# A decode block on one core: one load fewer for the first MLP weights, the last load of the second MLP weights cut in two

## The chip, the core and the metric

The kernel runs on one core of a Trainium2 chip. The core has a matrix engine (TensorE, PE in the rows), VectorE (DVE), ScalarE (ACT), GpSimd (POOL), a queue that issues transfers (SyncE, SP) and 16 DMA engines that move data from the chip's memory (HBM) into the on-chip buffer (SBUF). The metric is the time of one execution in device microseconds (us), as a median of several runs.

## The reference

One token for each of four sequences goes through attention over a window of the key and value cache, and then through an MLP; all data are float32.

```python
# x: (4, 1, 448); 16 query heads on 8 cached heads of width 256; the last 1024 cached positions
h  = x + attention(layernorm(x), k_cache, v_cache, wq, wo)
y  = layernorm(h)
g  = gelu(y @ w1 + b1)        # w1: (448, 1792)
h2 = h + (g @ w2 + b2)        # w2: (1792, 448)
```

## The kernel before

All caches and weights are packed by the host into a few wide arrays of 128 rows, one row for each SBUF partition, and are read once. The SP queue issues 23 loads in a fixed order (and one store at the end); the engines follow the data. Twelve wide loads, `stream0` to `stream11`, carry queries' weights, keys, values and output weights of the eight cached heads, in the order of the table `LOADS`, through a ring of three buffers. For each head the kernel projects the query, multiplies it with the keys (`scores`), takes the softmax, multiplies with the values (`values`), and adds the head's share of the output projection.

In the last pass of the loop over heads (`g == HKV - 1`) the last loads are issued: the last head's values `v7` in two parts, the output weights of the last two heads (`wo67`) and `w1` in three parts into the tile `tw`, and `w2` in four parts into the tile `tw2`. Each part has its own semaphore (DMAHW0 to DMAHW7 in turn), and an instruction that reads a part waits for that part's semaphore.

The tail of the program, after the attention, is a chain. The first layer is done in four steps `a` = 0 to 3 over 128 rows of `w1` each (the last step has 64 rows, and its weights lie side by side): `pu` collects `zT` times `w1`. `u` is then scaled, taken through the GELU on ScalarE, transposed into `put` and `gT`. The second layer runs over 14 chunks `c` of `w2`, 128 rows by 448 columns each: `py` collects `gT[:, c]` times chunk `c`. At the end `res` adds `py` and the rest, and `out` is stored.

TensorE's program order is written by hand. The weight parts before the change are: `w1` columns for `a` = 0 and 1 (1792 KB), for `a` = 2 (896 KB), for `a` = 3 (448 KB); `w2` chunks 0 to 7 (1792 KB), 8 to 10 (672 KB), 11 and 12 (448 KB), 13 (224 KB). `W1C` is `3 * F + F // 2` columns, `F` is 1792, `D` is 448, `H` is 64. Matmuls named `idle` (`keep_warm`) use constant data and only keep TensorE occupied.

Of the kernel before, what the change touches and what calls it, by code (L numbers as in the profile page):

```python
# [15 lines left out]
B, D = 4, 448  # L16
# [3 lines left out]
F = 1792  # L20
P = 128
H = P // 2
# [41 lines left out]
W1C = 3 * F + F // 2  # L64
# [1 line left out]
SCALE = DH ** -0.5  # L66

@with_exitstack
def block_kernel(ctx: ExitStack, tc, rows, first, streams, v7, wo67, w1, w2, out):
    nc = tc.nc  # L70
    const = ctx.enter_context(tc.tile_pool(name="const", bufs=1))
    ring = ctx.enter_context(tc.tile_pool(name="ring", bufs=3))
# [10 lines left out]
    def slot(name):  # L83
        return ring.tile([P, SLOT], F32, tag="t", name=name)
# [4 lines left out]
    def part(kind, g, i=0):  # L89
        while (kind, g, i) not in held:  # L90
            src = streams.pop(0)
            t = slot("stream")
            wanted = LOADS[len(LOADS) - len(streams) - 1]
            if src is streams_first:
                nc.sync.dma_start(t[:, : WC + X0], first)
            at = WC + X0 if src is streams_first else 0
            nc.sync.dma_start(t[:, at : at + src.shape[-1]], src)
            at = 0
            for one in wanted:
                held[one] = t[:, at : at + width(one)]  # L100
                at += width(one)
        return held[kind, g, i]

    def wq_parts(t):
        parts = [(a, a, slice(0, 512), t[:, a * 512 : (a + 1) * 512]) for a in range(3)]
        for i in range(2):
            parts.append((3, 3 + i, slice(i * 2 * P, (i + 1) * 2 * P), t[:, 3 * 512 : 4 * D]))
        return parts

    def wo_rows(t):  # L110
        return t.rearrange("p (j e) -> p j e", j=4)
# [11 lines left out]
    def load_v7():  # L123
        t = slot("v7")
        for a, b in ((0, V7A), (V7A, KV)):
            nc.sync.dma_start(t[:, a:b], v7[:, a:b])
        return chunk_pairs(t[:, :KV])
# [68 lines left out]
    def project_q(g, parts):  # L196
        pq = ps_m.tile([P, 512], F32, tag="m", name=f"pq{g}")
        for j, a, cols, w in parts:
            nc.tensor.matmul(pq[j * Q : (j + 1) * Q, cols], yT[:, a, :], w, start=True, stop=True)  # L199
        qs = work.tile([P, 512], F32, tag="qs", name=f"qs{g}")  # L200
        nc.scalar.copy(qs, pq)  # L201

        pt = ps_m.tile([P, 2 * REP, B], F32, tag="m", name=f"pqt{g}")
        for i in range(2 * REP):
            nc.tensor.matmul(pt[:, i, :], qs[:, i * P : (i + 1) * P], sel[:, :B], start=True, stop=True)  # L205

        src = pt.rearrange("p (r c) b -> p c b r", r=REP)
        for i in range(2):
            nc.vector.tensor_copy(qT[g % 2][:, :, :, i * REP : (i + 1) * REP], src)  # L209

    def scores(g):
        s = [ps_s.tile([P, 512], F32, tag="s", name=f"s{g}_{h}") for h in range(2)]
        if g == HKV - 1:
            keep_warm(12, s[0])
        mx = work.tile([P, 2], F32, tag="mx", name=f"mx{g}")
        for h in range(2):
            for c in range(2):
                for b in range(B):
                    nc.tensor.matmul(  # L219
                        s[h][b * Q : (b + 1) * Q, :], qT[g % 2][:, c, b, :], load_k(g, h, c)[:, b, :],  # L220
                        start=(c == 0), stop=(c == 1),
                    )
            nc.vector.reduce_max(mx[:, h : h + 1], s[h], axis=AX.X)  # L223
        nm = work.tile([P, 1], F32, tag="nm", name=f"nm{g}")
        nc.vector.tensor_max(nm, mx[:, 0:1], mx[:, 1:2])
        nc.vector.tensor_scalar_mul(nm, nm, -SCALE)  # L226
        p = work.tile([P, 2 * 512], F32, tag="p", name=f"p{g}")
        sums = work.tile([P, 2], F32, tag="sums", name=f"sums{g}")
        for h in range(2):
            nc.scalar.activation(  # L230
                p[:, h * 512 : (h + 1) * 512], s[h], AF.Exp, bias=nm, scale=SCALE,
                accum_out=sums[:, h : h + 1],
            )
        rec = work.tile([P, 1], F32, tag="rec", name=f"rec{g}")
        nc.vector.tensor_add(rec, sums[:, 0:1], sums[:, 1:2])
        nc.vector.reciprocal(rec, rec)
        return p, rec

    def transpose_p(g, p):
        pt = ps_t.tile([P, NKC, P], F32, tag="t", name=f"ppt{g}")  # L240
        if g == HKV - 1:
            keep_warm(8, pt.rearrange("p c k -> p (c k)"))
        for c in range(NKC):
            nc.tensor.transpose(pt[:, c, :], p[:, c * P : (c + 1) * P], ident)  # L244

        src = pt.rearrange("p (c i) (b q) -> p c i b q", i=2, b=B)
        for i in range(2):
            nc.vector.tensor_copy(pT[g % 2][:, :, :, i * REP : (i + 1) * REP], src[:, :, i, :, :REP])  # L248


    def values(g, v7=None):
        po = ps_o.tile([P, 2, DH], F32, tag="o", name=f"po{g}")
        for c in range(NKC // 2):
            vt = load_v(g, c) if v7 is None else v7[c]
            for b in range(B):
                nc.tensor.matmul(  # L256
                    po[b * Q : (b + 1) * Q], pT[g % 2][:, c, b, :], vt[:, :, b, :],
                    start=(c == 0), stop=(c == NKC // 2 - 1),
                )
        return po  # L260
# [5 lines left out]
    def columns(t, j):  # L266
        if j < 3:
            return t[:, j * P : (j + 1) * P].rearrange("p (i c) -> p i c", i=2)
        return t[:, None, 3 * P :].to_broadcast([t.shape[0], 2, H])
# [49 lines left out]
    def keep_warm(n, to=None):  # L319
        to = tail[0][:, 0, :] if to is None else to  # L320
        for _ in range(n):
            nc.tensor.matmul(to[:Q, :512], idle[:, :Q], idle, start=True, stop=True)  # L322
# [5 lines left out]
    for g in range(HKV):  # L328
        if g + 1 < HKV:
            p, rec_next = scores(g + 1)  # L330
            if g + 2 < HKV:
                project_q(g + 2, wq_parts(part("q", g + 2)))
            transpose_p(g + 1, p)
            if g + 1 == HKV - 2:
                keep_warm(8, ps_m.tile([P, 512], F32, tag="m", name="wait"))
            if g + 1 == HKV - 1:
                tail.append(ps_t.tile([P, 2, 512], F32, tag="t", name="tail"))
                accs = once.tile([P, D], F32, tag="u", name="accs")
                nc.scalar.copy(accs, acc)
                keep_warm(10)  # L340
                hsum = ps_s.tile([P, 512], F32, tag="s", name="hsum")[:, :P]
                ph = hsum.rearrange("p (i c) -> p i c", i=2)
                pu = ps_s.tile([P, 512], F32, tag="s", name="pu")[:, :FQ]
                for j in range(4):
                    nc.tensor.matmul(ph[j * Q : (j + 1) * Q], sel, columns(accs, j), start=True, stop=False)
        else:
            v7t = load_v7()
            tw = slot("w1")
            wo_last = [wo_rows(tw[:, i * WC : (i + 1) * WC]) for i in range(2)]
            nc.sync.dma_start(tw[:, : 2 * WC], wo67)  # L350
            tw1 = tw[:, 2 * WC : 2 * WC + W1C]
            for a, n in ((0, 2 * F), (2 * F, F), (3 * F, F // 2)):
                nc.sync.dma_start(tw1[:, a : a + n], w1[:, a : a + n])
            tw2 = slot("w2")
            for c0, n in ((0, 8), (8, 3), (11, 2), (13, 1)):
                nc.sync.dma_start(tw2[:, c0 * D : (c0 + n) * D], w2[:, c0 * D : (c0 + n) * D])
        if g == HKV - 1:
            keep_warm(4)
        po = values(g, v7t if g == HKV - 1 else None)
        heads(g, po, rec)  # L360
        if g < HKV - 2:
            project_o(g, wo_rows(part("o", g)))
        if g == HKV - 1:
            keep_warm(3)
            for i in range(2):
                project_o(HKV - 2 + i, wo_last[i])
        if g + 1 < HKV:
            rec = rec_next
# [5 lines left out]
    def w1_part(a, j):  # L374
        if a < 3:
            return slice(0, P), w1t[a][:, FQ * j : FQ * (j + 1)]
        rows = slice(H * (j // 2), H * (j // 2) + H)
        return rows, w1t[a][rows, FQ * (j % 2) : FQ * (j % 2 + 1)]
# [36 lines left out]
    for a in range(ND):  # L415
        for j in range(4):
            rows, w = w1_part(a, j)
# [27 lines left out]
    for c in range(NFC):  # L445
        for j in range(4):
            n = 2 if c == 0 or j < 3 else 1
# [79 lines left out]
```

## Time and profile before

| | before |
|---|---|
| median of 3 runs | 214.74 us (214.71 to 214.75) |
| the profiled execution's own time | 214.74 us |
| its span, first to last instruction | 212.9 us |
| PE busy | 148.6 us, 70% of the span |
| DVE, ACT, POOL busy | 33.5, 24.0, 5.6 us |
| DMA | 88.52 MB, mean 416 GB/s |
| chain that ended last | DMA 80%, PE 16%, DVE 1%, ACT 1% |

The profiled execution took as long as the median of the runs; 1.8 us of it lie outside the span. The chain that ended last is followed back from the last instruction to what each step waited for. Its line for DMA means that for 80% of the span the step that counted was a transfer on its way.

### The profile page before, as it was taken

What the parts mean: (1) busy time and instruction counts of PE and PEld (TensorE: products, weight loads), DVE (VectorE), ACT (ScalarE), POOL (GpSimd) and SP (SyncE); (2) the same over time, 40 slices, a digit from 0 to 9 for tenths busy, and PEclk for the clock granted to TensorE, in tenths of its full rate; (3) what the DMA queues carried; (4) which work ended last, traced back from release to release, by engine and by line L of the source; (5) the groups of instructions that cost most, each with busy time, mean ns of one, the idle gap of its engine ahead of it and who ended that gap; (6) DMA issues with size and microseconds to landing.
All of it is one profiled execution on the core that took longest, in us unless ns stands there. A gap on an engine that the chain in (4) does not pass through costs nothing.

```text
span 212.9 us, 2617 instructions
## 1 busy us (share of the span) xinstructions
PE 148.6 (70%) x1143; PEld 65.5 (31%) x1143; DVE 33.5 (16%) x138; ACT 24.0 (11%) x57; POOL 5.6 (3%) x17
## 2 busy tenths in 40 slices
PE   0476815842894895870798770687989898999984
PEld 0342311400421512330324130152352434426453
DVE  1410310400103100310104110031130031101220
ACT  1110300300002100210003000030030102000310
POOL 6100000000000000000000000000000000000110
PEclk9999985995559669997559996599699999999999
DMA  7999798999989999999999989999999999999991
GB/s 299 429 420 508 339 508 370 469 435 407 488 356 484 434 413 440 395 481 398 455 455 392 455 384 478 425 425 392 473 402 413 449 422 416 420 413 415 434 380 64
DMA packets 3499, 88.52 MB, mean 416 GB/s; under 512 B 400, under 2 KB 656, under 8 KB 1312
## 3 DMA queue, kind: packets, MB, share of 16 engines
q1 hardware_dynamic: 3456, 88.31, 96.9%
q8 instruction: 9, 0.15, 0.3%
q10 hardware_dynamic: 32, 0.05, 0.1%
q14 instruction: 2, 0.02, 0.0%
HBM read 88.29 MB, written 0.07 MB: 415 GB/s over the span
## 4 chain that ended last, share of the span: by engine, by line
DMA 80%; PE 16%; DVE 1%; ACT 1%; issue 1%; SPq 0%; ACTq 0%
DMA stream<-stream 60%; DMA w<-w 10%; DMA v<-v 9%; PE po L256 6%; PE s L219 4%; PE acc L293 1%; PE pot L281 1%; PE pq L199 1%; PE ppt L244 1%; DVE o L273 1%; ACT o L274 1%; PE pqt L205 1%; PE py L449 0%; ACT qs L201 0%; DVE oT L288 0%
## 5 line engine op out<-in xcount | busy, mean ns | idle before, releaser
L219 PE MATMUL s<-stream,qT 128*32 128x512 f32 x256 | 40.8, 788 | 18.6 <-DMA stream<-stream 18.6
L256 PE MATMUL po<-stream,pT 128*32 128x512 f32 x224 | 30.6, 685 | 15.6 <-DMA stream<-stream 15.4
L219 PEld LDWEIGHTS s<-stream,qT 128*32 128x32 f32 x256 | 10.5, 141 | 46.2 <-issue 33.7
L223 DVE TENSOR_REDUCE mx<-s 128x1 f32<-128x512 f32 x16 | 11.1, 692 | 63.7 <-PE s L219 63.7
L256 PEld LDWEIGHTS po<-stream,pT 128*32 128x32 f32 x224 | 7.2, 120 | 32.5 <-DMA stream<-stream 18.1
L281 PE MATMUL pot<-ident,o 128*128 128x8 f32 x64 | 11.3, 287 | 4.7 <-DVE o L273 3.7
L199 PE MATMUL pq<-stream,yT 128*32 128x512 f32 (+1 forms) x80 | 9.8, 582 | 6.0 <-DMA stream<-stream 3.1
L281 PEld LDWEIGHTS pot<-ident,o 128*128 128x128 f32 x64 | 9.9, 223 | 13.0 <-DVE o L273 11.3
L205 PE MATMUL pqt<-sel,qs 128*128 128x4 f32 x64 | 9.6, 274 | 6.0 <-ACT qs L201 6.0
L201 ACT COPY qs<-pq 128x512 f32<-128x512 f32 x8 | 4.7, 585 | 77.5 <-PE pq L199 77.5
L230 ACT ACTIVATE p<-s,nm 128x512 f32<-128x512 f32 x16 | 10.9, 688 | 17.4 <-DVE nm L226 17.4
L273 DVE TENSOR_SCALAR o<-po,rec 128x256 f32<-128x256 f32 x8 | 3.9, 484 | 53.8 <-PE po L256 53.8
L205 PEld LDWEIGHTS pqt<-sel,qs 128*128 128x128 f32 x64 | 8.9, 216 | 10.3 <-ACT qs L201 10.3
L274 ACT ACTIVATE o<-po,rec 128x256 f32<-128x256 f32 x8 | 3.8, 474 | 69.2 <-DVE o L273 69.2
L244 PE MATMUL ppt<-ident,p 128*128 128x128 f32 x64 | 9.8, 299 | 0.4 <-ACT p L230 0.4
L293 PE MATMUL acc<-stream,oT 128*32 128x448 f32 x48 | 7.6, 708 | 2.2 <-DVE oT L288 1.4
L322 PE MATMUL tail<-idle 128*32 128x512 bf16 x33 | 8.5, 381 | 0.4 <-DVE pT L248 0.4
L322 PEld LDWEIGHTS <-idle 128*32 128x32 bf16 x67 | 5.8, 96 | 9.3 <-issue 3.9
L244 PEld LDWEIGHTS ppt<-ident,p 128*128 128x128 f32 x64 | 8.1, 162 | 1.4 <-ACT p L230 1.1
L199 PEld LDWEIGHTS pq<-stream,yT 128*32 128x32 f32 x80 | 4.2, 122 | 13.6 <-issue 12.3
L193 POOL TENSOR_TENSOR r<-ve_r,mhalf 128x1 f32<-128x1 f32 x2 | 1.1, 542 | 191.8 <-DVE ve_r L192 191.8
L209 DVE COPY qT<-pqt 128x16 f32<-128x16 f32 x16 | 2.0, 170 | 17.6 <-PE pqt L205 17.6
(98 smaller groups left out, 70.0 us busy)
## 6 DMA issues: line engine op xcount, KB each, us to landing
stream<-stream SPq DMA_DIRECT2D x5, 7040.0 KB, 40.4
stream<-stream SPq DMA_DIRECT2D x2, 6912.0 KB, 39.8
stream<-stream SPq DMA_DIRECT2D x2, 4992.0 KB, 25.0
stream<-stream SPq DMA_DIRECT2D x2, 4096.0 KB, 24.1
stream<-stream SPq DMA_DIRECT2D x1, 5888.0 KB, 34.4
w<-w SPq DMA_DIRECT2D x2, 1792.0 KB, 23.1
v<-v SPq DMA_DIRECT2D x1, 3072.0 KB, 19.8
w<-wo SPq DMA_DIRECT2D x1, 1792.0 KB, 20.1
```

The costliest lines, as they stand in the source:

```text
L199: nc.tensor.matmul(pq[j * Q : (j + 1) * Q, cols], yT[:, a, :], w, start=True, stop=True)
L205: nc.tensor.matmul(pt[:, i, :], qs[:, i * P : (i + 1) * P], sel[:, :B], start=True, stop=True)
L219: nc.tensor.matmul(s[h][b * Q : (b + 1) * Q, :], qT[g % 2][:, c, b, :], load_k(g, h, c)[:, b, :], start=(c == 0), stop=(c == 1),)
L223: nc.vector.reduce_max(mx[:, h : h + 1], s[h], axis=AX.X)
L230: nc.scalar.activation(p[:, h * 512 : (h + 1) * 512], s[h], AF.Exp, bias=nm, scale=SCALE, accum_out=sums[:, h : h + 1],)
L244: nc.tensor.transpose(pt[:, c, :], p[:, c * P : (c + 1) * P], ident)
L256: nc.tensor.matmul(po[b * Q : (b + 1) * Q], pT[g % 2][:, c, b, :], vt[:, :, b, :], start=(c == 0), stop=(c == NKC // 2 - 1),)
L273: nc.vector.tensor_scalar_mul(o[:, 0], po[:, 0], rec)
L274: nc.scalar.mul(o[:, 1], po[:, 1], rec)
L281: nc.tensor.matmul(pt[:, c], o[:, i, c * P : (c + 1) * P], rows_of_pair[:, i * REP : (i + 1) * REP, :], start=(i == 0), stop=(i == 1),)
L293: nc.tensor.matmul(acc[i * Q : (i + 1) * Q, :], oT[g % 2][:, i, :], wt[:, i, :], start=(g == 0), stop=(g == HKV - 3),)
L322: nc.tensor.matmul(to[:Q, :512], idle[:, :Q], idle, start=True, stop=True)
```

## The change

The second and third part of `w1` become one load. The last part of `w2` (chunk 13) becomes two loads: its rows 0 to 63 from `w2` as before, and its rows 64 to 127 from a new array `w2e`, in which the host has laid these 64 rows as 8 blocks of 8 rows with an unused ninth row behind each block. The number of loads stays 23, and the bytes read stay the same.

```diff
-            for a, n in ((0, 2 * F), (2 * F, F), (3 * F, F // 2)):
+            for a, n in ((0, 2 * F), (2 * F, W1C - 2 * F)):
                 nc.sync.dma_start(tw1[:, a : a + n], w1[:, a : a + n])
             tw2 = slot("w2")
-            for c0, n in ((0, 8), (8, 3), (11, 2), (13, 1)):
+            for c0, n in ((0, 8), (8, 3), (11, 2)):
                 nc.sync.dma_start(tw2[:, c0 * D : (c0 + n) * D], w2[:, c0 * D : (c0 + n) * D])
+            nc.sync.dma_start(tw2[:H, 13 * D : 14 * D], w2[:H, 13 * D :])
+            nc.sync.dma_start(tw2[H:, 13 * D : 14 * D], w2e[:, :8, :])
...
+    w2e = np.concatenate([w2[H:, 13 * D :].reshape(8, 8, D), np.zeros((8, 1, D), np.float32)], axis=1)
```

On the SP queue, from the output weights to the end, the loads before were (`w_896` is the tile of `wo67` and `w1`, `w_901` that of `w2`; the shape is partitions by float32 elements, in brackets what the issue waits for):

```order
L350 DMA w_896<-wo 128x3584 [waits DMAHW4_49,PE_49]
L353 DMA w_896<-w 128x3584
L353 DMA w_896<-w 128x1792
L353 DMA w_896<-w 128x896
L356 DMA w_901<-w 128x3584 [waits DMAHW5_49,PE_49]
L356 DMA w_901<-w 128x1344
L356 DMA w_901<-w 128x896 [waits DMAHW6_49]
L356 DMA w_901<-w 128x448 [waits DMAHW7_49]
```

and with the change (`w_900` is the tile of `w2`):

```order
L350 DMA w_896<-wo 128x3584 [waits DMAHW4_49,PE_49]
L353 DMA w_896<-w 128x3584
L353 DMA w_896<-w 128x2688
L356 DMA w_900<-w 128x3584 [waits DMAHW5_49,PE_49]
L356 DMA w_900<-w 128x1344
L356 DMA w_900<-w 128x896
L357 DMA w_900<-w 64x448 [waits DMAHW6_49]
L358 DMA w_900<-w2e 64x1x448 [waits DMAHW7_49]
```

One issue is gone behind the first part of `w1`, all of `w2` moves up by one place, and two loads of 64 partitions stand at the end, with the waits that the two last loads had before.

On TensorE's queue, in the first layer, steps `a` = 2 and `a` = 3 of `pu` before, each with a wait of its own:

```order
L382 MATMUL tail<-zv,fold 128x1 [waits DVE_49,Activation_49]
L418 MATMUL pu<-w_896,zT 32x448 [waits DMAHW2_49]
L418 MATMUL pu<-w_896,zT 32x448 x3
L418 MATMUL pu<-w_896,zT 32x448 [waits DMAHW3_49]
L418 MATMUL pu<-w_896,zT 32x448 x3
```

and with the change:

```order
L384 MATMUL tail<-zv,fold 128x1 [waits DVE_49,Activation_49]
L420 MATMUL pu<-w_896,zT 32x448 [waits DMAHW2_49]
L420 MATMUL pu<-w_896,zT 32x448 x7
```

All eight matmuls now stand behind one wait, that for the joined load. Further on, the end of `py` on TensorE's queue before, from chunk 11 to the last chunk:

```order
L449 MATMUL py<-w_901,gT 32x128 [waits DMAHW6_49]
L449 MATMUL py<-w_901,gT 32x128 x2
L449 MATMUL py<-w_901,gT 32x64
L449 MATMUL py<-w_901,gT 32x128 [waits DVE_49]
L449 MATMUL py<-w_901,gT 32x128 x2
L449 MATMUL py<-w_901,gT 32x64
L449 MATMUL py<-w_901,gT 32x128 [waits DMAHW7_49]
L449 MATMUL py<-w_901,gT 32x128 x2
L449 MATMUL py<-w_901,gT 32x64
```

and with the change:

```order
L451 MATMUL py<-w_900,gT 32x128 [waits DMAHW5_49]
L451 MATMUL py<-w_900,gT 32x128 x2
L451 MATMUL py<-w_900,gT 32x64
L451 MATMUL py<-w_900,gT 32x128 [waits DVE_49]
L451 MATMUL py<-w_900,gT 32x128 x2
L451 MATMUL py<-w_900,gT 32x64
L451 MATMUL py<-w_900,gT 32x128 [waits DMAHW7_49,DMAHW6_49]
L451 MATMUL py<-w_900,gT 32x128 x2
L451 MATMUL py<-w_900,gT 32x64
```

The last chunk waits for two loads in place of one; nothing else on TensorE, VectorE, ScalarE or GpSimd changes its place.

## Rows read from the trace of the kernel before

**Rows 1.** Chain that ended last, its last pieces: start us, us, what.

```profile
187.47 21.49 DMA w<-w
208.96 0.04 issue
209.00 1.05 PE py L449 x12
210.05 0.02 issue
210.07 0.29 DVE res L453
```

**Rows 2.** Timeline of TensorE's weight loads in the second layer, 201 to 210.6 us.

```profile
206.28 2.36 PEld L449 LDWEIGHTS py<-w,gT 128*32 128x32 f32 x88 [0.76 <-issue]
209.00 0.37 PEld L449 LDWEIGHTS py<-w,gT 128*32 128x32 f32 x16 [0.35 <-DMA w<-w]
209.58 0.16 PEld L449 LDWEIGHTS py<-w,gT 128*32 128x32 f32 x8 [0.21 <-DMA w<-w]
```

**Rows 3.** Windows: per stretch PE, PEld, DVE, ACT, POOL busy, PEclk, DMA share, GB/s.

```profile
200.00:202.00 2.00, 2.00 (x20) 0.91 (x20) 0.38 (x2) 0.14 (x1) 0.54 (x1) 1.00 1.00 414
206.00:206.80 0.80, 0.49 (x22) 0.52 (x25) 0.14 (x1) 0.00 (x0) 0.00 (x0) 1.00 1.02 408
207.00:207.40 0.40, 0.40 (x24) 0.40 (x18) 0.00 (x0) 0.00 (x0) 0.00 (x0) 1.00 0.70 273
207.60:208.00 0.40, 0.40 (x25) 0.40 (x19) 0.00 (x0) 0.00 (x0) 0.00 (x0) 1.00 0.54 211
208.00:208.60 0.60, 0.60 (x30) 0.60 (x24) 0.00 (x0) 0.00 (x0) 0.00 (x0) 1.00 0.50 188
209.00:209.40 0.40, 0.40 (x16) 0.37 (x16) 0.00 (x0) 0.00 (x0) 0.00 (x0) 1.00 0.00 0
```

**Rows 4.** DMA queues: packets, MB, share of 16 engines' span.

```profile
q1 hardware_dynamic: 3456, 88.31, 96.9%
q8 instruction: 9, 0.15, 0.3%
```

**Rows 5.** Timeline of SP: start us, us, issues of the last loads, one window each.

```profile
174.53 1.38 SPq L353 DMA_DIRECT2D w<-w  x3
...
175.00 0.90 SPq L353 DMA_DIRECT2D w<-w  x2
...
183.95 0.80 SPq L356 DMA_DIRECT2D w<-w  x2
...
187.47 2.81 SPq L356 DMA_DIRECT2D w<-w  x2
...
189.95 0.33 SPq L356 DMA_DIRECT2D w<-w  x1
```

**Rows 6.** The same loads, one window each: KB, us from issue to landing.

```profile
w<-w SPq DMA_DIRECT2D x1, 1792.0 KB, 24.0
w<-w SPq DMA_DIRECT2D x1, 896.0 KB, 25.7
w<-w SPq DMA_DIRECT2D x1, 448.0 KB, 26.4
...
w<-w SPq DMA_DIRECT2D x1, 1792.0 KB, 22.2
w<-w SPq DMA_DIRECT2D x1, 672.0 KB, 23.5
...
w<-w SPq DMA_DIRECT2D x1, 448.0 KB, 21.5
w<-w SPq DMA_DIRECT2D x1, 224.0 KB, 19.6
```

**Rows 7.** Timeline, first layer's steps 2 and 3, 201.2 to 203.6 us.

```profile
201.29 0.30 PEld L382 LDWEIGHTS tail<-zv,fold 128*128 128x128 f32 x2 [0.73 <-issue]
201.60 0.16 PEld L418 LDWEIGHTS pu<-w,zT 128*32 128x32 f32 x8
202.49 0.15 PEld L418 LDWEIGHTS pu<-w,zT 64*32 64x32 f32 x8 [0.73 <-DMA w<-w]
203.51 0.48 DVE L431 SCALAR_TENSOR_TENSOR u<-pu,r,rs 128x256 f32<-128x256 f32 x1 [0.45 <-PE pu L418]
```

**Rows 8.** Timeline, VectorE's last copies before the second layer.

```profile
205.80 0.34 DVE L443 COPY gT<-put 64x8 f32<-64x8 f32 x2
```

**Rows 9.** Instructions of line 449: duration ns min/median/max, first and last start.

```profile
L449 PEldq EVENT_SEMAPHORE  x1: 51/51/51, 206.2 to 206.2; - x1
```

More of the change, by code (lines that the diff above doesn't have):

```diff
@@ L68, in block_kernel @@
 @with_exitstack
-def block_kernel(ctx: ExitStack, tc, rows, first, streams, v7, wo67, w1, w2, out):
+def block_kernel(ctx: ExitStack, tc, rows, first, streams, v7, wo67, w1, w2, w2e, out):
     nc = tc.nc
@@ L511 @@
         "rows": rows, "first": first, **streams, "v7": v[-1], "wo67": np.concatenate([wo[-2], wo[-1]], axis=1), "w1": w1, "w2": w2,
+        "w2e": w2e,
     }
```

## The prediction

> **What bounds the kernel now.** I read the chain that ended last first: its final link is a load of `w2` weights that lands at 208.96 us, then 1.05 us of TensorE in the second layer, then VectorE's `res` at 210.07 [rows 1]. So the end is set by the last weight loads, and the timeline of TensorE's weight loads shows by how much [rows 2]: 88 loads (chunks 0 to 10; 8 to a chunk) run from 206.28 without a pause that counts and end at 208.65 (209.00 less the 0.35 us that the engine then sat idle for a load); 16 (chunks 11, 12) go from 209.00 to 209.37; after 0.21 us of idleness the last 8 (chunk 13) begin at 209.58, when the last load has landed. Two waits of 0.35 and 0.21 us are all that the last loads cost TensorE. That 0.21 us, and a little of the 0.35, is what the change can win.
>
> Next I read the DMA share in narrow stretches of the tail [rows 3]. It is 1.00 and 1.02 until 206.8 us, 0.70 at 207.0 to 207.4, 0.54 at 207.6 to 208.0, 0.50 from 208.0 to 208.6, and 0.00 from 209.0. A share of 0.50 is 8 of 16 engines: half of them finish at about 207 to 208, the other half work on to about 209.0, and these alone decide when the last loads land. A reason that fits stands among the queues: besides the data there are nine packets of instructions, which took 0.3% of 16 engines' span, so 0.003 x 16 x 212.9 / 9 = 1.1 us of one engine each [rows 4]. One such packet on each of eight engines would make them late by about as much as is seen.
>
> The times of landing come from the issues and their us to landing [rows 5, 6]. `w1`: steps 0 and 1 at 174.53 + 24.0 = 198.53; step 2 at 175.00 + 25.7 = 200.70; step 3 at 175.47 (the end of the three issues, 175.91, less one issue of about 0.43) + 26.4 = 201.87. `w2`: 183.95 + 22.2 = 206.15; about 184.35 + 23.5 = 207.85; 187.47 + 21.5 = 208.97; 189.95 + 19.6 = 209.55. The last two agree with the ends of TensorE's waits.
>
> **The change, step by step.**
>
> *One load less in `w1`.* The differences of those landings price a load: 896 KB took 2.17 us, 448 KB took 1.17 and 1.12, 224 KB took 0.58. Twice 1.12 less 2.17 is 0.07 us that a load costs whatever its size; from 1.17 it would be 0.17, from 0.58 against 1.12 it is 0.04. I take 0.07 (0.04 to 0.17). The joined load lands at 201.80, and all of `w2` lands 0.07 earlier: chunks 0 to 7 at 206.08, chunks 11 and 12 at 208.90. Nothing changes for SP: the moved issues keep their waits, stand 18 us and more ahead of their landings, and the two last keep the places of the two last.
>
> *A wait for step 2.* Before, its weights landed at 200.70, ahead of TensorE, which came to them at 201.60 after the two weight loads of the `zv` mean [rows 7]. Now they land with step 3's at 201.80; 0.04 us pass from a landing to the start [rows 1], so step 2 starts at 201.84, 0.24 us late (with no saving by the joined load 0.31; never below nothing). Behind it stand step 3, whose own weights were there, and then `u`: VectorE took it up at 203.51, when `pu` was done [rows 7], so `u`, the GELU, `put` and `gT` all move by 0.24. `gT`'s last copy ended at 206.14 [rows 8], and TensorE began `py` at 206.28; that becomes 206.52, its weights being there at 206.08.
>
> *Where that goes.* The 88 loads of chunks 0 to 10 take 2.37 us, so they end at 208.89. Chunks 11 and 12 are there at 208.94 (208.90 and 0.04). The idle 0.35 us has swallowed the delay, with 0.05 to spare. Were that cover gone, each further tenth would be paid at the end. The 16 loads then end at 208.94 + 0.37 = 209.31, against 209.37 before.
>
> *The last chunk.* Its 224 KB took 0.58 us on 16 engines. Rows 0 to 63 go as half the bytes with the whole fixed cost, about (0.58 - 0.07) / 2 + 0.07 = 0.33. Rows 64 to 127, if eight engines share them, are as many rows for each of the eight as the whole load had before: 0.58 on these eight, nothing on the others. No row says which eight are late. If the late eight are the ones that get nothing of rows 64 to 127, they are done at 208.90 + 0.33 = 209.23 (before 209.55). The early eight ended their data by 208.0; less 0.07 and 0.26, plus 0.58, that is 208.25, and with the half microsecond between the end of the data at 209.0 and the landing at 209.55 they land at 208.8. So chunk 13 is there at 209.23, earlier than TensorE, which comes at 209.31. Its first matmul now waits for two loads: a semaphore wait of its own took 51 ns on this queue [rows 9], at most 0.05 more. I take 209.36 for the start, against 209.58: 0.22 us earlier. From there the 8 loads, `res`, the store and the end are as before.
>
> The sum: 214.74 - 0.22 = **214.52 us**, made against the profiled execution, whose own time equals the median of the runs.
>
> Bounds of this case: with 0.17 for the fixed cost chunks 11 and 12 start at 208.84, end at 209.21, and without the semaphore's 0.05 the gain is 0.37 (214.37). With 0.04, the step-2 delay is 0.27, `py`'s 88 loads end at 208.92, the next start at 208.97 and end at 209.34, and with the semaphore's 0.05, and as much again for anything the split costs on top, the gain is 0.14 (214.60).
>
> A rule that speaks against the second edit: the Trainium skill, "DMA: Bandwidth & Descriptors", Rules for kernel authors, advises against two transfers to disjoint partition halves, because both run over all 16 engines and so serialize; one load of 128 partitions is better. By it the last chunk would cost 0.33 twice instead of 0.58. No run here shows it. The same page (Why a DMA increments its semaphore by 16 and not by 1) lets the engines be counted by the largest number up to 16 that divides the slowest dimension on both sides, here 64 and 8, so 8, the lowest-numbered ones; no row here shows that either.
>
> **The rivals.**
>
> *The late eight, or one of them, share rows 64 to 127.* Slower. One late engine is enough, since the chunk waits for the last. They land at 208.90 + 0.33 + 0.58 = 209.81, chunk 13 starts at 209.85, 0.27 later than now (0.28 with 0.04 as the fixed cost, 0.22 with 0.17, and 0.05 more with the semaphore's wait). The time is 215.01 (214.96 to 215.07). For it: nothing in the profile names the engines. Against it: if the lateness comes from queues of their own, as the packets of instructions suggest, the late eight may well be one block, and then it is wholly the one block or the other. The point that decides: whether an engine still busy at 208.6 has rows of the second part.
>
> *The eight blocks run over all 16 engines.* The change then does not do what it says. The halves cost 0.33 each, and the chunk lands at 208.90 + 0.66 = 209.56, as before, whatever the fixed cost, since one is saved and one added: 214.75 (214.80 with the semaphore's wait). The rule on halves of the Trainium skill's page "DMA: Bandwidth & Descriptors", above, would make it this. Against it stands only that the two sides of the second load are cut differently, 64 rows on one, 8 blocks on the other.
>
> *One engine moves all 64 rows.* 0.58 us for 8 rows is about 0.07 a row, so 64 take 4.6 us. An early engine starts them by 208.0 - 0.33, ends at 212.3 and lands at about 212.8, a late one a microsecond later: 3.3 to 4.3 us on the end, 218.0 to 219.0. Nothing in the rows speaks for it; no load before had blocks on one side and rows on the other.
>
> **How the numbers follow.** Forecast (late eight relieved): 0.53; it is a judgement of the two blocks, not a reading. Late ones loaded: 0.30. All 16: 0.10. One engine: 0.04. Something the rows don't show: 0.03. The likeliest gives 214.52, with a range of its own from 214.37 to 214.60. Forecast and first rival together have no more than 0.83, so the range for 8 in 10 takes in both: 214.37 to 215.08. A measurement of this kernel can tell about 0.2% (0.43 us) from no change. Forecast, first rival and second all lie inside that; only one engine, and part of the unseen, lie outside. The unseen and a stronger gain than the bounds give faster 0.06, the single engine and a worse delay slower 0.08, and the same 0.86.
>
> **What would show it.** Right: DMA share falls from 0.5 to nothing a quarter of a microsecond earlier; TensorE's wait before the last 8 loads of `py` is under 0.06; step 2 waits for `w1` by about a quarter of a microsecond and the idleness before chunk 11 shrinks from 0.35 to about 0.05. Wrong: the last wait grows to about 0.5, with a share of 0.5 or less to past 209.2 (late ones loaded); a share of 0.06 for microseconds (one engine); no idleness before chunk 11 and a later `py` (the joined load costs more than its cover). It would also fail if a different half were late in another execution.

## The result and the profile after

The change makes the kernel slower: 215.29 us as median of 11 runs (215.21 to 215.57), against 214.75 (214.65 to 215.44) for the kernel before on the same chip; the ratio is 1.0025 [1.0017, 1.0033]. That is 0.54 us more, where I forecast 0.22 less, and outside my range (to 215.08).

The profiled execution of the changed kernel took 215.33 us. Its chain ended last in this way (start us, us, what):

```profile
207.41 3.30 PE py L451 x66
210.71 0.02 issue
210.73 0.29 DVE res L455
```

Against [rows 1], `res` comes 0.66 us later, and the load has gone from the chain: TensorE now seems to be the bound. Its timeline of weight loads says the same, against [rows 2]:

```profile
202.99 0.16 PEld L420 LDWEIGHTS pu<-w,zT 128*32 128x32 f32 x8
...
207.38 3.02 PEld L451 LDWEIGHTS py<-w,gT 128*32 128x32 f32 x112 [0.46 <-issue]
```

This is a trap. The first layer runs 1.4 us late (202.99 against 201.60 in [rows 7]), so all 112 loads of `py` find their weights there. In this execution TensorE's granted clock stood at half of its full level for some microseconds from 187.6 us on (last section). Executions of the kernel before with as low a mean clock (0.840 to 0.848, where the others have about 0.86) took 215.45 to 215.51 us (four of them), those of the change 215.33 to 215.57 (three): as far as these few tell, the two kernels don't differ with that stretch, so TensorE's rows of this trace can't show what the change did. A second profile of the same kernel, without that stretch, shows it (run `ra_change_again`; timeline of weight loads, and of `res`):

```profile
201.87 0.16 PEld L420 LDWEIGHTS pu<-w,zT 128*32 128x32 f32 x8 [0.23 <-DMA w<-w]
...
206.26 1.71 PEld L451 LDWEIGHTS py<-w,gT 128*32 128x32 f32 x64 [0.46 <-issue]
208.33 0.59 PEld L451 LDWEIGHTS py<-w,gT 128*32 128x32 f32 x24 [0.36 <-DMA w<-w]
209.61 0.62 PEld L451 LDWEIGHTS py<-w,gT 128*32 128x32 f32 x24 [0.70 <-DMA w<-w]
...
210.55 0.29 DVE L455 TENSOR_TENSOR res<-py,hb 128x128 f32<-128x128 f32 x1 [4.14 <-PE py L451]
```

Read it against [rows 2]. Chunks 8 to 10, which ran on without a wait before, now wait 0.36 us for their load. Chunks 11 and 12 start at 209.61, not 209.00. Chunk 13, the one whose load was cut, no longer waits at all: the last 24 loads go in one piece. So the time was lost on loads that the change doesn't touch, ahead of the cut one. The windows of the same profile answer to [rows 3] (columns as there):

```profile
206.00:206.80 0.80, 0.51 (x22) 0.54 (x26) 0.40 (x3) 0.00 (x0) 0.00 (x0) 1.00 1.02 408
207.00:207.40 0.40, 0.40 (x24) 0.40 (x17) 0.00 (x0) 0.00 (x0) 0.00 (x0) 1.00 0.86 211
207.60:208.00 0.40, 0.40 (x22) 0.37 (x13) 0.00 (x0) 0.00 (x0) 0.00 (x0) 1.00 0.51 148
208.00:208.60 0.60, 0.51 (x22) 0.27 (x17) 0.00 (x0) 0.00 (x0) 0.00 (x0) 1.00 0.62 224
209.00:209.40 0.40, 0.18 (x6) 0.00 (x0) 0.00 (x0) 0.00 (x0) 0.00 (x0) 1.00 0.46 135
```

At 207.0 the engines are busier than before (0.86 against 0.70) and move less (211 GB/s against 273). Busy share times 16 counts the busy engines; GB/s over that count tells at what pace each of them runs. That is 211 / (0.86 x 16) = 15.3 GB/s for each, against 273 / (0.70 x 16) = 24.4 before; at 207.6 it is 18.1 against 24.4. The engines are slower than before.

### The profile page after: what moved, and what is told of

It is laid out like the page before. It is cut to its first block, busy times and chain, and to the rows that moved or that the text cites. A ratio compares the mean times of both kernels' runs of the same rounds, so it can differ in the third digit from the quotient of the medians.

```text
span 213.5 us, 2618 instructions
## 1 busy us (share of the span) xinstructions
PE 150.6 (71%) x1143; PEld 66.2 (31%) x1143; DVE 33.5 (16%) x138; ACT 24.1 (11%) x57; POOL 5.6 (3%) x17
## 4 chain that ended last, share of the span: by engine, by line
DMA 58%; PE 34%; another core or an unknown queue 3%; DVE 1%; ACT 1%; issue 1%; SPq 0%; ACTq 0%
DMA stream<-stream 49%; PE s L219 9%; DMA v<-v 9%; PE po L256 8%; PE pot L281 3%; PE acc L293 3%; PE tail L322 2%; PE pu L420 2%; PE py L451 2%; PE pq L199 1%; PE pqt L205 1%; DVE o L273 1%; PE ppt L244 1%; PE hsum L299 1%
## 5 line engine op out<-in xcount | busy, mean ns | idle before, releaser
L219 PE MATMUL s<-stream,qT 128*32 128x512 f32 x256 | 38.5, 749 | 16.9 <-DMA stream<-stream 16.9
L256 PE MATMUL po<-stream,pT 128*32 128x512 f32 x224 | 32.3, 721 | 17.1 <-DMA stream<-stream 17.0
L219 PEld LDWEIGHTS s<-stream,qT 128*32 128x32 f32 x256 | 10.0, 135 | 42.5 <-issue 33.2
L199 PE MATMUL pq<-stream,yT 128*32 128x512 f32 (+1 forms) x80 | 10.9, 642 | 5.5 <-DVE yT L313 2.9
L205 PE MATMUL pqt<-sel,qs 128*128 128x4 f32 x64 | 10.1, 281 | 6.1 <-ACT qs L201 6.1
L205 PEld LDWEIGHTS pqt<-sel,qs 128*128 128x128 f32 x64 | 9.4, 225 | 11.0 <-ACT qs L201 11.0
L256 PE MATMUL po<-v,pT 128*32 128x512 f32 x32 | 5.3, 825 | 0.5 <-DMA v<-v 0.5
## 6 DMA issues: line engine op xcount, KB each, us to landing
stream<-stream SPq DMA_DIRECT2D x2, 4992.0 KB, 23.9
stream<-stream SPq DMA_DIRECT2D x2, 4096.0 KB, 23.9
w<-w SPq DMA_DIRECT2D x2, 1792.0 KB, 23.1
```

Source lines behind the costliest of these rows:

```text
L219: nc.tensor.matmul(s[h][b * Q : (b + 1) * Q, :], qT[g % 2][:, c, b, :], load_k(g, h, c)[:, b, :], start=(c == 0), stop=(c == 1),)
L256: nc.tensor.matmul(po[b * Q : (b + 1) * Q], pT[g % 2][:, c, b, :], vt[:, :, b, :], start=(c == 0), stop=(c == NKC // 2 - 1),)
```

## The experiments

All runs in one table; start times of chunks 11/12 and of chunk 13 and of `res` are from the profiles, "after res" is the end of the span less the start of `res`, both read from the trace to 0.001 us. The row of `g1_w1_to_low` has its times from `g1_again`. The ratio is to the kernel before on the same chip, which was 214.75 or 214.76 us each time.

| kernel | loads | chunks 11, 12 | chunk 13 | res | after res | median us | ratio [95%] |
|---|---|---|---|---|---|---|---|
| before | 23 | 209.00 | 209.58 | 210.07 | 2.80 | 214.75 | |
| the change (second profile) | 23 | 209.61 | no wait | 210.55 | 2.81 | 215.29 | 1.0025 [1.0017, 1.0033] |
| e1_join_only | 22 | 209.06 | 209.65 | 210.14 | 2.70 | 214.66 | 0.9996 [0.9987, 1.0005] |
| e2_split_only | 24 | 209.67 | 210.19 | 210.71 | 2.87 | 215.46 | 1.0033 [1.0020, 1.0045] |
| d0_spare_low | 24 | 209.27 | 209.98 | 210.48 | 2.87 | 215.13 | 1.0013 [1.0004, 1.0022] |
| d1_spare_high | 24 | 209.59 | 210.27 | 210.77 | 2.87 | 215.47 | 1.0032 [1.0019, 1.0045] |
| f1_spare_low_by_4 | 25 | 209.04 | 209.61 | 210.10 | 2.95 | 214.94 | 1.0005 [0.9997, 1.0013] |
| k1_spare_high_by_4 | 25 | 209.81 | 210.66 | 211.15 | 2.96 | 215.89 | 1.0048 [1.0031, 1.0065] |
| f2_spare_low_far | 24 | 209.26 | 209.91 | 210.40 | 2.86 | 215.10 | 1.0015 [1.0006, 1.0024] |
| f4_change_by_4 | 24 | 209.78 | no wait | 210.71 | 2.88 | 215.47 | 1.0030 [1.0021, 1.0039] |
| h_plain_halves | 24 | 209.56 | 210.12 | 210.62 | 2.86 | 215.35 | 1.0025 [1.0015, 1.0034] |
| g1_w1_to_low | 24 | 209.19 | 209.75 | 210.24 | 2.87 | 215.03 | 1.0007 [0.9997, 1.0018] |

**Each edit alone.** `e1_join_only` joins the `w1` parts and leaves `w2` as it was; `e2_split_only` does the split alone. Against the change, first `e1_join_only`, then `e2_split_only`:

```diff
-            for c0, n in ((0, 8), (8, 3), (11, 2)):
+            for c0, n in ((0, 8), (8, 3), (11, 2), (13, 1)):
...
-            nc.sync.dma_start(tw2[:H, 13 * D : 14 * D], w2[:H, 13 * D :])
-            nc.sync.dma_start(tw2[H:, 13 * D : 14 * D], w2e[:, :8, :])
```

```diff
-            for a, n in ((0, 2 * F), (2 * F, W1C - 2 * F)):
+            for a, n in ((0, 2 * F), (2 * F, F), (3 * F, F // 2)):
```

> Only the first edit: parts two and three of the first MLP weights in one load, chunk 13 in one load as before. Theory A (the split of chunk 13 slows the transfers around it: from 207.6 to 208.0 us the changed kernel moved 193 GB/s at a DMA share of 0.69, 17.5 GB/s for a busy engine, against 211 at 0.54, 24.4, before): no loss here, 214.65 to 214.80 us. Theory B (the joined load holds up step 2 of the first layer and with it the second layer): the loss of 0.5 us is here, 215.2. Theory C (late engines simply get more rows): as A here.

> Only the second edit: chunk 13 in two loads of 64 partitions, the second in 8 blocks; the first MLP weights in three loads as before. Theory A: the whole loss, 215.1 to 215.4 us, with 17 to 18 GB/s for a busy engine after 207.4 us. Theory B: 214.5 to 214.8. Theory C: 215.0, and 23 to 24 GB/s for a busy engine as before, since then only the number of rows is at fault.

The whole loss is in the split (215.46), and none in the join (214.66, no difference that can be measured). Weight loads of `e1_join_only`:

```profile
201.97 0.16 PEld L418 LDWEIGHTS pu<-w,zT 128*32 128x32 f32 x8 [0.22 <-DMA w<-w]
...
206.36 2.36 PEld L449 LDWEIGHTS py<-w,gT 128*32 128x32 f32 x88 [0.46 <-issue]
209.06 0.37 PEld L449 LDWEIGHTS py<-w,gT 128*32 128x32 f32 x16 [0.34 <-DMA w<-w]
209.65 0.16 PEld L449 LDWEIGHTS py<-w,gT 128*32 128x32 f32 x8 [0.22 <-DMA w<-w]
```

Step 2 waits 0.22 us, yet the idleness ahead of `py` shrinks from 0.76 to 0.46, and the two waits at the end are as in [rows 2]. The delay has gone ahead of `py`. Weight loads of `e2_split_only`:

```profile
208.28 0.59 PEld L451 LDWEIGHTS py<-w,gT 128*32 128x32 f32 x24 [0.28 <-DMA w<-w]
209.67 0.37 PEld L451 LDWEIGHTS py<-w,gT 128*32 128x32 f32 x16 [0.81 <-DMA w<-w]
210.19 0.19 PEld L451 LDWEIGHTS py<-w,gT 128*32 128x32 f32 x8 [0.15 <-DMA w<-w2e]
```

**A spare load behind the kernel before.** The same 64 rows in 8 blocks of 8 are loaded once more, behind all others, into a tile that nothing reads: `d0_spare_low` to partitions 0 to 63, `d1_spare_high` to 64 to 127.

```diff
+            spare = const.tile([P, D], F32, name="spare")
+            nc.sync.dma_start(spare[:H, :], w2e[:, :8, :])
```

(`spare[H:, :]` in `d1_spare_high`.)

> The kernel before, with one load more at the very end of the queue, which nothing waits for before the end: 64 rows in 8 blocks of 8 into partitions 0 to 63 of a spare tile. Theory A, in the form that the early eight engines get in the way of the late eight by writing to partitions 64 to 127: no loss, 214.7 to 214.85 us. Theory C (late engines get more rows): no loss either, as nothing waits for these rows.

> The same, with the spare rows written to partitions 64 to 127. Theory A in that form: the last weight loads land 0.2 to 0.5 us later than before, and a busy engine moves fewer GB/s between 207.4 and 208.6 us than the 24 of before; 214.95 to 215.3 us. Theory C, and theory A in a form in which the partitions don't matter: the same time as with the spare rows in partitions 0 to 63.

Weight loads of `d0_spare_low`, then of `d1_spare_high`:

```profile
209.27 0.37 PEld L451 LDWEIGHTS py<-w,gT 128*32 128x32 f32 x16 [0.61 <-DMA w<-w]
209.98 0.16 PEld L451 LDWEIGHTS py<-w,gT 128*32 128x32 f32 x8 [0.34 <-DMA w<-w]
```

```profile
209.59 0.37 PEld L451 LDWEIGHTS py<-w,gT 128*32 128x32 f32 x16 [0.91 <-DMA w<-w]
210.27 0.16 PEld L451 LDWEIGHTS py<-w,gT 128*32 128x32 f32 x8 [0.31 <-DMA w<-w]
```

No instruction of the kernel reads the spare rows, and still they cost 0.37 and 0.71 us, by making the loads ahead of them late. For `d0_spare_low` both theories had no loss, so both fail there; theory A in its form about partitions 64 to 127 keeps only the difference between the two runs. The records of the landings tell more: a load's semaphore rises once for each engine that has finished its share, 16 times for a load of 128 partitions, and the trace holds each time, but not which engine it was. The spare load has eight landings, so eight engines share it. The eight of the first spare load in `f1_spare_low_by_4` (below) all come by 209.42 us, before the five latest of chunk 13 (209.43 to 209.57). If each engine takes its loads in the order of the queue, these five have no share. My rivals with all 16 and with one engine are out.

**Place or pattern.** `f1_spare_low_by_4` writes the same spare rows to partitions 0 to 63 as two loads of 8 blocks of 4 rows; `k1_spare_high_by_4` is the same with partitions 64 to 127; `f2_spare_low_far` is `d0_spare_low` with its source rows 25 KB apart.

First the load of `f1_spare_low_by_4` (`k1_spare_high_by_4` adds `H` to the partitions), then that of `f2_spare_low_far`:

```diff
+            for i in range(2):
+                nc.sync.dma_start(spare[i * Q : (i + 1) * Q, :], w2e[i, :, :4, :])
```

```diff
+            nc.sync.dma_start(spare[:H, :], w2e[:, :8, 13 * D :])
```

> As the kernel with the spare rows in partitions 0 to 63 (215.13 us), but in two loads of 32 partitions, each in 8 blocks of 4 rows, so that each engine writes 4 neighbouring partitions and then the 4 that lie 32 higher. Theory A1 (engines collide where they write: partitions 4 apart from each other in turn, as in blocks of 8, bring two engines to one place): the loss goes, 214.7 to 214.85 us. Theory A2 (the reads of rows that lie close together in memory collide): the same loss as in blocks of 8, 215.0 to 215.2.

> The spare rows in two loads of 32 partitions, each in 8 blocks of 4 rows, as in the run by 4 into partitions 0 to 63 (214.94 us, the last weights on time), but into partitions 64 to 127. If the place of writing alone decides (theory A1: the late eight engines are held up by others that write to partitions 64 to 127), 215.3 to 215.5 us with the last weights 0.4 to 0.7 us late. If what the early engines do beside the late ones does not depend on the place, as by 4 into 0 to 63: 214.9 to 215.0.

> As the kernel with the spare rows in partitions 0 to 63 in 8 blocks of 8, but the rows lie 25 KB apart in memory, as those of the second MLP weights do, and not next to each other. Theory A1 (collision where they write): the same loss, 215.0 to 215.2 us. Theory A2 (collision where they read): 214.7 to 214.85.

`f1_spare_low_by_4`, weight loads and `res`, then windows:

```profile
209.04 0.37 PEld L452 LDWEIGHTS py<-w,gT 128*32 128x32 f32 x16 [0.37 <-DMA w<-w]
209.61 0.16 PEld L452 LDWEIGHTS py<-w,gT 128*32 128x32 f32 x8 [0.20 <-DMA w<-w]
...
210.10 0.29 DVE L456 TENSOR_TENSOR res<-py,hb 128x128 f32<-128x128 f32 x1 [3.94 <-PE py L452]
```

```profile
207.60:208.00 0.40, 0.40 (x23) 0.40 (x18) 0.00 (x0) 0.00 (x0) 0.00 (x0) 1.00 0.68 260
208.00:208.60 0.60, 0.60 (x30) 0.60 (x26) 0.00 (x0) 0.00 (x0) 0.00 (x0) 1.00 0.59 221
```

`k1_spare_high_by_4`, the same two views:

```profile
208.32 0.59 PEld L452 LDWEIGHTS py<-w,gT 128*32 128x32 f32 x24 [0.29 <-DMA w<-w]
209.81 0.37 PEld L452 LDWEIGHTS py<-w,gT 128*32 128x32 f32 x16 [0.91 <-DMA w<-w]
210.66 0.16 PEld L452 LDWEIGHTS py<-w,gT 128*32 128x32 f32 x8 [0.48 <-DMA w<-w]
...
211.15 0.29 DVE L456 TENSOR_TENSOR res<-py,hb 128x128 f32<-128x128 f32 x1 [4.96 <-PE py L452]
```

```profile
207.60:208.00 0.40, 0.40 (x23) 0.40 (x15) 0.00 (x0) 0.00 (x0) 0.00 (x0) 1.00 0.88 188
208.00:208.60 0.60, 0.58 (x24) 0.31 (x19) 0.00 (x0) 0.00 (x0) 0.00 (x0) 1.00 0.64 179
```

The two kernels differ in the partitions written and in nothing else. Written low, the loads run beside the others at full pace (260 / (0.68 x 16) = 23.9 GB/s for each busy engine) and no weight is late by more than 0.04 us. Written high, each busy engine moves 13.4, and `res` is 1.05 us later. So the place of writing decides. The place of reading makes no such difference, as far as it was tried: with `f2_spare_low_far` `res` is within 0.08 us of `d0_spare_low`. The cutting matters too: in the low half one load of 8-row blocks delays chunks 11 and 12 by 0.27 (`d0_spare_low`), two loads of 4-row blocks by 0.04.

**The change with 4-row blocks, and with plain halves.** `f4_change_by_4` cuts rows 64 to 127 of the change into two loads of 8 blocks of 4. `h_plain_halves` keeps the `w1` parts of before and loads chunk 13 as two plain halves from `w2`, without blocks.

`f4_change_by_4` against the change, then `h_plain_halves` against `e2_split_only`:

```diff
-            nc.sync.dma_start(tw2[H:, 13 * D : 14 * D], w2e[:, :8, :])
+            for i in range(2):
+                nc.sync.dma_start(tw2[H + i * Q : H + (i + 1) * Q, 13 * D : 14 * D], w2e[i, :, :4, :])
```

```diff
-            nc.sync.dma_start(tw2[H:, 13 * D : 14 * D], w2e[:, :8, :])
+            nc.sync.dma_start(tw2[H:, 13 * D : 14 * D], w2[H:, 13 * D :])
```

> The changed kernel with rows 64 to 127 in two loads of 32 partitions, each in 8 blocks of 4 rows, in place of one in 8 blocks of 8. Theory A1: part of the loss goes, as engines no longer meet each other in this load, but they still write where the late engines write; 214.85 to 215.1 us. Theory A2: the loss stays, 215.2 to 215.4.

> The kernel before with chunk 13 in two plain loads, rows 0 to 63 and rows 64 to 127, without blocks, so that 16 engines share each of them. Two things can be seen: whether the first half, which stands in the changed kernel too, costs anything by itself. Theory A1 (16 engines write to 64 partitions, so two meet at one place): the loads take about twice as long, the last weights land 0.2 to 0.5 us later, 215.0 to 215.3 us. If a half in itself is harmless: 214.75 to 214.9.

`f4_change_by_4` gains nothing (215.47), where I had expected part of the loss to go: its rows still go to the high half. And no special pattern is needed to lose: plain halves cost 0.60 us (215.35), with engines about as slow at 207.0 as in the change, 202 / (0.80 x 16) = 15.8 GB/s for each:

```profile
207.00:207.40 0.40, 0.40 (x24) 0.40 (x18) 0.00 (x0) 0.00 (x0) 0.00 (x0) 1.00 0.80 202
```

**Trying for a faster version.** `g1_w1_to_low` takes work from the late engines without touching `w2`: of `w1`'s last rows, three quarters of the columns go to partitions 0 to 63 instead of half, two of the quarters by 4-row blocks. `g1_again` is a second profile of it and `ra_change_again` the second profile of the change.

```diff
-            for a, n in ((0, 2 * F), (2 * F, F), (3 * F, F // 2)):
+            for a, n in ((0, 2 * F), (2 * F, F + FQ)):
...
+            for i in range(2):
+                nc.sync.dma_start(tw1[i * Q : (i + 1) * Q, 3 * F + FQ :], w1e[i, :, :4, :])
```

> The kernel before, with another cure for the late eight engines: of the last 64 rows of the first MLP weights (two halves of the columns in partitions 0 to 63 and 64 to 127 before), three quarters of the columns lie in partitions 0 to 63 and one quarter in 64 to 127. One quarter each comes in the load of part two, which takes it in; the other two quarters come in two loads of 32 partitions, each in 8 blocks of 4 rows. The late engines move 8 rows of 1792 bytes less each, the early ones as many more. Theory A1: no collision, the last weights land 0.4 to 0.55 us earlier and the second layer runs almost without waits: 214.2 to 214.45 us. Theory A2, or any theory by which eight-block loads slow their neighbours wherever they write: no gain, 214.75 to 215.3.

> The changed kernel once more for another profile, since in the profiled execution TensorE's granted clock was at half from 187.6 to 191.0 us. In an execution without that stretch the joined load, not the clock, sets step 2, chunks 11 and 12 are waited for until about 209.6, the last chunk until about 209.95, and the time is 215.2 to 215.3 us.

> The kernel with three quarters of the last first-layer rows in partitions 0 to 63 once more, for a profile without the stretch at half clock (187.6 to 191.0 us). The last weights should land at about 209.15 us as in the first profile; if nothing else is in the way the second layer ends 0.4 us earlier than before, 214.3 us. The 12 timed runs gave 215.03, so something else must be seen in it: a later first layer, or a longer end.

No gain: 215.03 us, where 214.2 to 214.45 was expected. Weight loads in `g1_again`:

```profile
209.19 0.37 PEld L452 LDWEIGHTS py<-w,gT 128*32 128x32 f32 x16 [0.36 <-DMA w<-w]
209.75 0.16 PEld L452 LDWEIGHTS py<-w,gT 128*32 128x32 f32 x8 [0.19 <-DMA w<-w]
```

The landings say why. Before, the last five landings of chunk 13 lie between 209.44 and 209.53 us, and three more at 209.04 to 209.13. In `g1_again` the last two are at 209.66 and 209.71, all others by 209.09. The late five were indeed relieved by about 0.45, but two of the engines that took over their work were themselves only 0.4 us ahead of the last before, and now end the chunk. No version here beats the kernel before clear of the noise.

## Why the prediction was wrong

**The step that failed** is the term for rows 64 to 127, "0.58 on these eight, nothing on the others", and with it "all of `w2` lands 0.07 earlier" for all chunks behind 7. I priced a load of half the partitions by its rows for each engine and took the engines as independent. In `ra_change_again` the four earliest landings of rows 0 to 63 are at 207.10 to 207.47, those of rows 64 to 127 at 208.23 to 208.32: paired in this order, about 1.0 us for the term of 0.58. And the others did not get "nothing". The landings (us; records of the semaphores in the three traces) show what took its place:

```
                 w1 step 0,1   w1 last   chunks 0-7   8-10     11,12    13
before             198.56      201.87     206.18     207.84   208.96   209.53
e1_join_only       198.69      201.93     206.25     207.95   209.02   209.61
ra_change_again    198.57      201.83     206.14     208.28   209.57   210.00
```

With the change, chunks 8 to 10 come 0.44 us later and chunks 11 and 12 0.61 later; with the join alone both come at most 0.11 later. Engines that are early begin their share of the half loads while others still carry the chunks ahead, and these are slowed. `f1_spare_low_by_4` against `k1_spare_high_by_4` shows that this hangs on the partitions written to. The Trainium skill, "SBUF — State Buffer", section "Door 1: The DMA port swizzle (why `[64,N]` ≈ `[32,N]`)", has a rule that fits: bandwidth depends on how many of 16 ports the partitions reach; four neighbouring partitions share one, partition + 32 is on the same port, + 64 on another, and in a load of 128 partitions each engine serves a port of its own, eight of them the low half's. By it, if the eight engines of the second load are the low half's, the change sends them to the ports that the other eight are still writing through; plain halves put 16 engines on eight ports; 8-row blocks in the low half meet each other pairwise, 4-row blocks don't. The paces from 207 to 209 us agree. Windows of the kernel before, `f1_spare_low_by_4`, `d0_spare_low`, `f2_spare_low_far`, `d1_spare_high` and `k1_spare_high_by_4`, in this order:

```profile
207.00:209.00 2.00, 1.92 (x70) 1.65 (x61) 0.00 (x0) 0.00 (x0) 0.00 (x0) 1.00 0.56 212
207.00:209.00 2.00, 1.94 (x70) 1.67 (x61) 0.00 (x0) 0.00 (x0) 0.00 (x0) 1.00 0.73 270
207.00:209.00 2.00, 1.93 (x70) 1.66 (x61) 0.00 (x0) 0.00 (x0) 0.00 (x0) 1.00 0.73 241
207.00:209.00 2.00, 1.92 (x70) 1.65 (x61) 0.00 (x0) 0.00 (x0) 0.00 (x0) 1.00 0.76 260
207.00:209.00 2.00, 1.96 (x69) 1.56 (x59) 0.00 (x0) 0.00 (x0) 0.00 (x0) 1.00 0.75 229
207.00:209.00 2.00, 1.98 (x70) 1.61 (x62) 0.00 (x0) 0.00 (x0) 0.00 (x0) 1.00 0.79 238
```

That is 23.7, 23.1, 20.6, 21.4, 19.1 and 18.8 GB/s for each busy engine. (Windows of 0.4 us scatter more: from 207.6 to 208.0 `d0_spare_low` has 15.3 and `f2_spare_low_far`, with the same delays, 21.0.) The ports themselves stand in no record, so the dependence on the half is shown and the ports as its reason are not. It is the rule I should have weighed; the one I did weigh, that of the Trainium skill's page "DMA: Bandwidth & Descriptors" (Rules for kernel authors) that halves serialize, is too mild: by it plain halves would cost 0.33 twice in place of 0.58, 0.08 us more, and they cost 0.60.

**The choice between the blocks of engines** (0.53 against 0.30) took the late eight to be one block, wholly with or wholly without a share of rows 64 to 127. The landings show neither. In `f1_spare_low_by_4` the landings of the spare loads follow those of chunk 13 in steps of about 0.3 us, and by these steps six of the late eight (the eight last landings) have no share and two have one. A reason is in the landings of the kernel before: the packets of instructions seem to make engines late, as the prediction supposed, but one engine at a time. In the load that ends at 101.62 us 3 engines land within half a microsecond of the last; behind the packets at 122.47, 146.77, 170.78, 191.25 and 202.55 us (1.0 to 1.1 us each) there are 4, 5, 6, 7 and 8. That the forecast's case came closer is luck: with the change the last landing of rows 64 to 127 is at 209.93, just ahead of 210.00 for rows 0 to 63. The wait before the last 8 loads of `py` vanished. From the landing of chunks 11 and 12 to that of chunk 13 it is 0.43 us where it was 0.57. I expected 0.33. That 0.14 is all that the split wins, against 0.61 lost ahead of it. The net, 0.47, agrees with the shift of `res` (210.07 to 210.55) and lies, like the 0.54 between the medians, inside the interval of 0.37 to 0.71 us.

**One load less** saves what I took: between the landing of the first part of `w1` and that of its last, 3.31 us before and 3.24 with the join, 0.07 less; to chunks 11 and 12, 10.40 and 10.33.

**The wait for step 2** came as predicted, 0.23 us (forecast 0.24). Where it goes was misread: I let it move the start of `py` to 206.52 and be swallowed before chunk 11. It was swallowed sooner. `py`'s first matmul before and with the change (timeline of TensorE, the kernel before and then `ra_change_again`):

```profile
206.31 0.53 PE L449 MATMUL py<-w,gT 128*32 128x128 f32 x12 [0.69 <-DMA w<-w]
```

```profile
206.29 0.53 PE L451 MATMUL py<-w,gT 128*32 128x128 f32 x12 [0.39 <-DVE gT L443]
```

It had waited for the weights of chunks 0 to 7 (landed at 206.18), and needs only the first copy of `gT` (line 443 in the changed kernel, 441 before), not the two later ones of [rows 8]. The size of the cover was wrong, its effect on the end nothing.

**The spread** was too narrow for a reason: every case I priced left the loads ahead of the split alone. The chance of 0.08 for slower rested on a single engine and on "a worse delay", to which no row had given a price.

**Left open.** Why 8-row blocks in the low half also delay chunks 11 and 12, which by the landings hang on engines not among the eight (209.27 against 209.00), isn't settled by these runs. Nor is why blocks of 4 rows do better than blocks of 8 in the low half and worse in the high half (`res` at 211.15 in `k1_spare_high_by_4`, 210.77 in `d1_spare_high`).

## What to carry to other kernels

A small load at the end of a queue isn't priced by its own bytes alone: engines that finish early start it while others still carry the load ahead. Here these were slowed most when the small load went to partitions 64 to 127. Look at GB/s for each busy engine (GB/s over share times 16) in the windows around a cut load; a fall there, with the loads ahead landing later, points to contention and not to more work. To test it, load the same bytes into a tile that nobody reads, once to each half of the partitions.

## What was not expected of the hardware

**The number of loads moves the end of the program.** From `res` to the end of the span it is 2.70 us with 22 loads, 2.80 and 2.81 with 23, 2.86 to 2.88 with 24, 2.95 and 2.96 with 25. This accounts for 0.15 of the 0.19 us of `f1_spare_low_by_4`, whose weights were on time. It is no price of a load. The store lands 1.87 to 1.89 us behind the start of `res` in all of them. At the end SP waits for the semaphores of the transfers in a fixed order, in five waits about 0.06 us apart, and the store takes the semaphore that is next in turn. With 22 loads that is the one in the fifth wait, with 23 in the third, with 24 in the second and with 25 in the first, so 0, 2, 3 and 4 waits still follow when the store has landed.

**A stretch at half clock.** In the first profile of the change the granted clock, 1.00 before, is at 0.50 (1.2 of 2.4 GHz) at 188 to 190 us. Windows of that profile:

```profile
185.00:188.00 3.00, 2.47 (x15) 1.37 (x19) 0.19 (x1) 0.00 (x0) 0.00 (x0) 0.93 0.97 407
188.00:190.00 2.00, 2.00 (x12) 0.49 (x8) 0.00 (x0) 0.00 (x0) 0.00 (x0) 0.50 1.06 445
190.00:192.00 2.00, 2.00 (x20) 0.72 (x16) 0.00 (x0) 0.00 (x0) 0.00 (x0) 0.75 0.96 402
```

and of the kernel before in the same place:

```profile
185.00:188.00 3.00, 2.43 (x15) 1.33 (x19) 0.19 (x1) 0.01 (x1) 0.00 (x0) 1.00 1.00 420
188.00:190.00 2.00, 2.00 (x24) 0.65 (x20) 0.00 (x0) 0.00 (x0) 0.00 (x0) 1.00 1.03 435
```

TensorE (first figure behind the length) was about as busy from 185 to 188 us in both (2.47 and 2.43 of 3 us), so these rows don't tell what makes the clock fall. The first profile of `g1_w1_to_low` has the same stretch, from 187.6 to 191.0 us. In the change's first profile the last head's 32 matmuls with `v` take 5.32 us, in the kernel before 3.64.
